# Chunked attention and a sine MLP on one core: two stages one after the other, rewritten as an interleaved sequence

## The chip, the cores and the metric

The kernel runs on one NeuronCore of a Trainium2 chip. The metric is device time in microseconds (us) of one execution, taken over several runs; beside it stands one profiled execution, whose trace gives each instruction's start and duration on the engines: PE (TensorE, matrix products; PEld is its loading of weights), ACT (ScalarE, activation functions and copies), DVE (VectorE, elementwise work), POOL (GpSimd, here memsets, copies and the issue of DMAs) and SP (SyncE, the issue of DMAs).

## What is computed

Four batches, eight heads, 768 positions, head size 64. Queries are taken in chunks of 32; a chunk sees the keys from 16 positions before it to 8 behind it, and 8 memory keys of its head. The attention's output, 3072 tokens of 512 features, goes through a two-layer network with a sine in the middle.

```python
for c in range(24):                               # chunks of 32
    q_c = q[:, :, 32*c : 32*c+32]
    k_full = concat([mem_k, k[:, :, max(0, 32*c-16) : min(768, 32*c+40)]])
    v_full = concat([mem_v, v[:, :, max(0, 32*c-16) : min(768, 32*c+40)]])
    a = exp(q_c @ k_full.T / 8 - max); a = a / a.sum()
    out[:, :, 32*c : 32*c+32] = a @ v_full
x = out as 3072 x 512
h = x @ w_in                                      # 512 -> 2048
g = h + sin(alpha * h)**2 / alpha
y = g @ w_out                                     # 2048 -> 512
```

Inputs and output are float32; the products run in bfloat16.

## The kernel before

Work on the attention goes by blocks of 96 queries, three chunks; 96 queries see 120 keys, which with the 8 memory keys are exactly 128 partitions. So one product of a 128-column window of `kTi` (keys, transposed) with 96 columns of `qT_all` (queries, transposed) gives the scores of one head and block with the keys on the partitions. Which of the three chunks may see which key is put in by six more rows of the contraction: rows 64 to 69 of `qT_all` and `kTi` hold patterns (`qft`, `kgit`, built in lines 69 to 124) whose product adds 256 where a key is allowed, and the Exp (L237) takes 32 away again after scaling.

`prep_head` (L147 to L219) loads one head of one batch in float32, most of it from SP, the middle of the values from POOL (L204, L208, L214). VectorE casts queries and keys (L157, L177, L178); TensorE transposes them in pieces of 128 or 96 (L160, L180, L183 to L185) into two PSUM tiles `t1`, `t2`; ScalarE copies them out (L161, L186, L190, L194); VectorE copies the memory keys (L195) and the pattern rows (L165, L199) and casts the values (L218). `attn_block` (L221 to L260) does a block: per four heads four score products (L231), one Exp of 384 columns (L237), four products with the values (L244), a reciprocal and a multiplication (L248, L249), then four transposes to put features on the partitions (L257) and a copy into `xT_store` (L260), which holds all 3072 tokens.

Behind the four batches comes the MLP, in six blocks of 512 tokens. For each of 16 tiles of 128 hidden features: four matmuls (L303) into `hT`, Sin on ScalarE (L310), the square on ScalarE (L316) or VectorE (L320) in turn, and the last step on VectorE (L323), which reads `hT` again. `hT` has three buffers. Then, for each 128 tokens, 16 matmuls (L331), a copy by ScalarE (L338) and a store from SP (L339).

The order of the instructions on each engine is set by the Tile scheduler, from priorities that follow the program's order. The MLP's pools are opened only when the attention's are closed, so its PSUM is the attention's PSUM.

Of the kernel before, what the change touches and what calls it, by code (L numbers as in the profile page):

```python
# [9 lines left out]
CHUNK = 32  # L10
BIG = 256.0
EXP_BIAS = -32.0
P = 128
QW = 96


def _bf16_tile(pool, shape, name, **kw):
    return pool.tile(shape, mybir.dt.bfloat16, name=name, **kw)


def _f32_tile(pool, shape, name, **kw):
    return pool.tile(shape, mybir.dt.float32, name=name, **kw)
# [3 lines left out]
def kernel(  # L26
# [16 lines left out]
    assert D == 64 and H * D == d_model and d_model == 512 and d_ff % P == 0  # L43
    assert S % QW == 0 and S % P == 0 and S % 192 == 0 and NM == 8
    NJ = S // QW
    NQB = S // P
    NTOK = B * S
    FT = d_ff // P
    KT = d_model // P
    NPOS = S  # L50
    KCOLS = 16 + NPOS + 8 * 9
    NSEG = 9
    scale = 1.0 / 8.0

    consts = ctx.enter_context(tc.tile_pool(name="consts", bufs=1))

    ident = _bf16_tile(consts, [P, P], "ident")
    masks.make_identity(nc, ident[:])

    bias_exp = _f32_tile(consts, [P, 1], "bias_exp")  # L60
    nc.vector.memset(bias_exp[:], EXP_BIAS)

    qft = _bf16_tile(consts, [P, NPOS], "qft")
    kgit = _bf16_tile(consts, [P, KCOLS], "kgit")

    tmp_stack = ExitStack()
    pattmp = tmp_stack.enter_context(tc.tile_pool(name="pattmp", bufs=1))

    qf0 = _bf16_tile(pattmp, [6, NPOS], "qf0")
    nc.gpsimd.memset(qf0[:], 0.0)  # L70
    qf_view = qf0[:].rearrange("p (a m r) -> p a m r", a=NPOS // 192, m=6, r=32)
    nc.gpsimd.affine_select(
        out=qf_view, in_=qf_view, compare_op=mybir.AluOpType.not_equal,
        fill=BIG, base=0, pattern=[[0, NPOS // 192], [1, 6], [0, 32]],
        channel_multiplier=-1,
    )
    kg0 = _bf16_tile(pattmp, [6, NPOS], "kg0")
    nc.gpsimd.memset(kg0[:], 0.0)
    kg_view = kg0[:].rearrange("p (a u) -> p a u", a=NPOS // 192, u=192)
    nc.gpsimd.affine_select(  # L80
        out=kg_view, in_=kg_view, compare_op=mybir.AluOpType.is_ge, fill=1.0,
        base=-40, pattern=[[0, NPOS // 192], [1, 192]], channel_multiplier=-32,
    )
    nc.gpsimd.affine_select(
        out=kg_view, in_=kg_view, compare_op=mybir.AluOpType.is_ge, fill=0.0,
        base=16, pattern=[[0, NPOS // 192], [1, 192]], channel_multiplier=-32,
    )
    kgC = kg0[:, 192:NPOS].rearrange("p (a u) -> p a u", a=NPOS // 192 - 1, u=192)
    nc.gpsimd.affine_select(
        out=kgC, in_=kgC, compare_op=mybir.AluOpType.is_ge, fill=1.0,  # L90
        base=152, pattern=[[0, NPOS // 192 - 1], [1, 192]], channel_multiplier=-32,
    )
    kgD = kg0[:, 0:NPOS - 192].rearrange("p (a u) -> p a u", a=NPOS // 192 - 1, u=192)
    nc.gpsimd.affine_select(
        out=kgD, in_=kgD, compare_op=mybir.AluOpType.is_gt, fill=1.0,
        base=176, pattern=[[0, NPOS // 192 - 1], [-1, 192]], channel_multiplier=32,
    )
    kgi = _bf16_tile(pattmp, [6, KCOLS], "kgi")
    nc.gpsimd.memset(kgi[:], 0.0)
    nc.vector.tensor_copy(kgi[:, 16:24], kg0[:, 0:8])  # L100
    for s in range(1, 8):
        nc.vector.tensor_copy(
            kgi[:, 32 + 104 * (s - 1):32 + 104 * (s - 1) + 96],
            kg0[:, 8 + 96 * (s - 1):8 + 96 * s],
        )
    nc.vector.tensor_copy(kgi[:, 760:848], kg0[:, 680:768])
# [263 lines left out]
```

## Time and profile before

| | us |
|---|---|
| median of 3 runs | 392.58 |
| lowest, highest | 391.58, 392.81 |
| span of the profiled execution, first to last instruction | 391.8 |
| PE busy in it | 300.2 |
| DVE busy | 230.6 |
| ACT busy | 199.4 |
| POOL busy | 78.1 |

No separate time is listed for the profiled execution; its span is 391.8, 0.8 below the median of the runs, and that much is taken to lie around it. How to read what follows: in a group, `L310 ACT ACTIVATE u<-hT,alpha_sb` is the instruction of line 310 on ScalarE that writes `u` from `hT` and `alpha_sb`, with shapes and count; then busy us, mean ns of one, then the engine's idle time just before them and what ended it. A timeline row has start, duration, engine, line, and how many are merged. A row of windows has, for a stretch, the busy time and count of PE, PEld, DVE, ACT and POOL, the granted clock, the mean busy share of the DMA engines, and GB/s. DMA rows have the size and the median time from issue to landing. `SPq` and `POOLq` are the queues from which SP and POOL issue.

### The profile page before, as it was taken

The page shows a single profiled execution, that of the slowest core. Times are in us where ns is not written, and L with a number is a line of the kernel's source. Part 1 is how long each engine was busy: PE and PEld are TensorE (multiplying, and loading weights), DVE is VectorE, ACT ScalarE, POOL GpSimd, SP SyncE. Part 2 cuts the span into 40 slices and gives each one's busy share as a digit, 9 for nine tenths or more (in the row PEclk, how much of TensorE's full clock was granted, in tenths as well). Part 3 has the DMA queues.
Part 4 walks back from the last instruction along what each step waited for, and adds up shares of the span by engine and source line. Part 5 has one row for each costly group of instructions (what it writes and reads, how often), then busy time and mean ns, then how long its engine had stood idle before and what let it go on. Part 6 is the DMA issues. An engine that isn't in the chain of part 4 may idle for free.

```text
span 391.8 us, 5738 instructions
## 1 busy us (share of the span) xinstructions
PE 300.2 (77%) x1908; PEld 177.6 (45%) x1924; DVE 230.6 (59%) x707; ACT 199.4 (51%) x362; POOL 78.1 (20%) x115
## 2 busy tenths in 40 slices
PE   0245543975577956598588999999999999999996
PEld 0134432853455734486474344444444444444442
DVE  6988213578455788467273970880870870871860
ACT  0334442643446634474554863863863763763761
POOL 9835302003453442624100000000000000000000
PEclk9999999999999999999999999999999999999999
DMA  5977999913597455855200002002002002002002
GB/s 134 174 133 123 205 194 190 155 31 72 117 174 133 90 104 124 152 114 119 43 2 0 0 2 105 3 3 107 0 2 107 0 2 107 1 2 108 0 13 96
DMA packets 66989, 31.73 MB, mean 81 GB/s; under 512 B 59152, under 2 KB 61200, under 8 KB 66960
## 3 DMA queue, kind: packets, MB, share of 16 engines
q1 hardware_dynamic: 60272, 19.75, 24.7%
q0 software_dynamic: 6688, 11.62, 14.4%
q8 instruction: 15, 0.25, 0.3%
q14 instruction: 14, 0.11, 0.1%
HBM read 29.24 MB, written 6.29 MB: 91 GB/s over the span
## 4 chain that ended last, share of the span: by engine, by line
PE 51%; ACT 17%; DVE 13%; DMA 9%; issue 4%; POOL 3%; SPq 2%; another core or an unknown queue 0%; DVEq 0%; ACTq 0%; POOLq 0%
PE ops_t L331 19%; PE hT L303 12%; ACT u L310 5%; DMA k_stage<-in_k_dram 5%; PE out L244 5%; DVE gT L323 4%; DMA v_stage<-in_v_dram 4%; PE t L160 4%; ACT s L316 4%; PE t L183 4%; PE ps L231 3%; ACT kTi L190 2%; ACT qT_all L161 2%; ACT pT L237 2%; PE xtp L257 2%
## 5 line engine op out<-in xcount | busy, mean ns | idle before, releaser
L323 DVE SCALAR_TENSOR_TENSOR gT<-s,inv_alpha,hT 128x512 bf16<-128x512 f32 x96 | 71.2, 747 | 63.7 <-ACT s L316 61.5
L303 PE MATMUL hT<-xT_store,w_in_sb 128*128 128x512 bf16 x375 | 94.8, 385 | 5.6 <-DVE gT L323 3.6
L331 PE MATMUL ops_t<-w_out_sb,gT 128*128 128x512 bf16 x377 | 89.3, 379 | 0.4
L310 ACT ACTIVATE u<-hT,alpha_sb 128x512 f32<-128x512 f32 x96 | 64.6, 679 | 18.4 <-PE hT L303 16.6
L303 PEld LDWEIGHTS <-w_in_sb 128*128 128x128 bf16 x384 | 38.0, 99 | 56.2 <-issue 15.7
L331 PEld LDWEIGHTS <-gT 128*128 128x128 bf16 x384 | 37.0, 98 | 46.2 <-DVE gT L323 4.7
L160 PE MATMUL t<-ident,q_bf 128*64 128x128 bf16 x192 | 26.2, 309 | 24.1 <-DVE kTi L195 21.8
L161 ACT COPY qT_all<-t 64x768 bf16<-64x768 bf16 x32 | 25.3, 792 | 36.4 <-PE t L160 36.3
L237 ACT ACTIVATE pT<-ps,bias_exp 128x384 bf16<-128x384 f32 x64 | 35.4, 577 | 14.9 <-PE ps L231 11.3
L244 PE MATMUL out<-Vwin,pT 128*96 128x65 bf16 x256 | 35.1, 269 | 7.6 <-ACT pT L237 5.3
L204 POOL DMA_DIRECT2D v_stage<-in_v_dram x32 | 21.5, 671 | 95.0 <-DVE Vwin L218 59.3
L338 ACT COPY o_sb<-ops_t 128x512 f32<-128x512 f32 x24 | 14.0, 585 | 49.8 <-PE ops_t L331 47.6
L231 PE MATMUL ps<-qT_all,kTi 70*128 70x96 bf16 x256 | 35.9, 276 | 3.5 <-DVE kTi L195 2.0
L320 DVE TENSOR_TENSOR s<-u 128x512 f32<-128x512 f32 x48 | 32.8, 684 | 5.0 <-ACT u L310 5.0
L190 ACT COPY kTi<-t 64x576 bf16<-64x576 bf16 x32 | 20.2, 632 | 25.8 <-PE t L185 25.8
L160 PEld LDWEIGHTS <-q_bf 128*64 128x64 bf16 x192 | 20.9, 162 | 27.6 <-issue 20.1
L244 PEld LDWEIGHTS <-pT 128*96 128x96 bf16 x256 | 28.0, 188 | 11.1 <-ACT pT L237 8.9
L208 POOL DMA_DIRECT2D v_stage<-in_v_dram x32 | 28.5, 889 | 14.2 <-DMA w_out_sb<-in_moe_w_out_dram 12.7
L316 ACT ACTIVATE s<-u 128x512 f32<-128x512 f32 x48 | 30.2, 630 | 1.5
L180 PE MATMUL t<-ident,k_bf 96*64 96x96 bf16 x64 | 10.9, 270 | 25.3 <-DVE k_bf L178 13.8
L231 PEld LDWEIGHTS <-kTi 70*128 70x128 bf16 x256 | 23.9, 137 | 8.6 <-issue 4.3
L183 PE MATMUL t<-ident,k_bf 96*64 96x96 bf16 x192 | 20.9, 276 | 7.9 <-ACT kTi L186 7.6
(59 smaller groups left out, 275.8 us busy)
## 6 DMA issues: line engine op xcount, KB each, us to landing
q_stage<-in_q_dram SPq DMA_DIRECT2D x32, 192.0 KB
out_dram<-o_sb SPq DMA_DIRECT2D x24, 256.0 KB
k_stage<-in_k_dram SPq DMA_DIRECT2D x32, 168.0 KB
v_stage<-in_v_dram POOLq DMA_DIRECT2D x32, 168.0 KB, 4.2
w_in_sb<-in_moe_w_in_dram POOLq DMA_DIRECT2D x1, 2048.0 KB, 15.8
w_out_sb<-in_moe_w_out_dram POOLq DMA_DIRECT2D x1, 2048.0 KB, 28.7
v_stage<-in_v_dram POOLq DMA_DIRECT2D x32, 42.0 KB, 3.0
k_stage<-in_k_dram SPq DMA_DIRECT2D x32, 22.0 KB
```

The source lines that it names most:

```text
L160: nc.tensor.transpose(t1[:, jb, :], q_bf[:, jb, :], ident[:])
L161: nc.scalar.copy(qT_all[0:64, h, 0:NPOS].rearrange("p (j c) -> p j c", j=NQB), t1[:, 0:NQB, :],)
L183: nc.tensor.transpose(t2[:, s - 3, 0:QW], k_bf[:, s, :], ident[0:QW, 0:QW])
L231: nc.tensor.matmul(ps4[:, e, :], kTi[0:70, h, 104 * j:104 * j + P], qT_all[0:70, h, QW * j:QW * j + QW],)
L237: nc.scalar.activation(pT4[:], ps4[:], mybir.ActivationFunctionType.Exp, bias=bias_exp[:], scale=scale,)
L244: nc.tensor.matmul(og[0:QW, e, :], pT4[:, e, :], Vwin[:, h, j, :])
L303: nc.tensor.matmul(hT[:, :], w_in_sb[:, kt, ft * P:(ft + 1) * P], xT_store[:, kt, tokbase:tokbase + TB], start=(kt == 0), stop=(kt == KT - 1),
L310: nc.scalar.activation(u[:], hT[:], mybir.ActivationFunctionType.Sin, scale=alpha_sb[:, ft:ft + 1],)
L316: nc.scalar.activation(s2[:], u[:], mybir.ActivationFunctionType.Square,)
L320: nc.vector.tensor_tensor(out=s2[:], in0=u[:], in1=u[:], op=mybir.AluOpType.mult,)
L323: nc.vector.scalar_tensor_tensor(out=gT[:, ft, :], in0=s2[:], scalar=inv_alpha[:, ft:ft + 1], in1=hT[:], op0=mybir.AluOpType.mult, op1=myb ...
L331: nc.tensor.matmul(ops_t[:, :], gT[:, ft, s * P:(s + 1) * P], w_out_sb[:, ft, :], start=(ft == 0), stop=(ft == FT - 1),)
```

## The change

The kernel is rewritten; line numbers of the new one are given here as N.

- Order. `tc.manual_schedule()` makes each engine run its instructions in the order in which the code writes them. Attention of batch 0 comes first ("burst"). Then, for each batch i, the first product of its MLP ("L1": 16 tiles over all 768 tokens, N297 to N318), and after it the attention of batch i+1 mixed with the second product of batch i ("L2", N320 to N339). L2 is a Python generator that yields after each matmul; `Stream.take(n)` emits n of them. Within a burst, a step emits the scores and Exps of one block, then some matmuls of L2, the product with the values of an earlier block (1 block earlier, 4 in the first mixed burst, 2 in batch 0's), more of L2, and the transposes of the block before that. What is left of L2 goes two matmuls per tile into the next L1, and the rest behind it.
- Preparation. Loads cast from float32 to bfloat16 on the way and are all issued from POOL. Two heads lie side by side: VectorE puts a pair together (`pair_up`, N193), one transpose of 128 by 128 serves both, six for keys (`t_k`) and six for queries (`t_q`) of a pair; position 6a+r of a head comes out as column a of transpose r, so the copies out of PSUM read with a step of 128 elements. The queries go to `qz`, whose first half has the odd head's rows at zero and whose second half the even head's, so that one product with 192 columns gives both heads' scores. The preparation of batch i+1 is written into L1 of batch i, one half pair every second tile.
- Masks. The pattern rows go. Each block has three Exps, one per chunk of 32 queries for all eight heads (256 columns), with a bias per partition that is -30000 for keys that the chunk does not see (`biasm`).
- Values. They are loaded by block and not by head, two DMAs for a block, into `vws`; the memory rows are copied in by POOL (`put_memv`), the memory keys likewise (`put_memk`).
- PSUM. `big`, two buffers of two banks, serves scores and `hT` (now 128 by 768, two halves of 384); `opp`, one bank, the output of L2; `atp`, three banks, the rest. In the last L2 every second output tile takes a bank of `atp`.
- MLP. L1 has 8 matmuls of 384 columns per tile; the square is on VectorE in every second tile of batch 0 and in every fourth of the others. The outputs are copied in turn by VectorE and ScalarE.
- Weights. `w_in` comes in eight DMAs and `w_out` in four, behind the values of batch 0.

PE, in the attention of a later batch. Before, scores and value products stand among the transposes of the next batch's preparation (`t` tiles):

```order
L184 MATMUL t_2114<-ident,k_bf 64x24
L185 LDWEIGHTS memk_bf
L185 MATMUL t_2114<-ident,memk_bf 64x8
L257 LDWEIGHTS x_blk
L257 MATMUL xtp<-ident,x_blk 128x96
```

Now, in the second burst: `sc` are the scores, `o` the output of L2 of the batch before, `ot` the product with the values.

```order
L233 MATMUL sc<-qz,kTi 128x192
L327 LDWEIGHTS gT
L327 MATMUL o<-w_out_sb,gT 128x512
L327 LDWEIGHTS gT
L327 MATMUL o<-w_out_sb,gT 128x512
L327 LDWEIGHTS gT
L327 MATMUL o<-w_out_sb,gT 128x512
L261 LDWEIGHTS pt_99
L261 MATMUL ot<-vw_88,pt_99 128x65
```

Matmuls of the MLP now stand between those of the attention.

POOL, near the start. Before, its share of the value loads begins among the pattern constants:

```order
L112 AFFINE_SELECT sel<-sel 6x70 [waits Pool_49]
L204 DMA v_stage<-in_v_dram 24x7x64
L89 AFFINE_SELECT kg_75<-kg_75 6x576 [waits Pool_49]
L208 DMA v_stage<-in_v_dram 96x7x64
L94 AFFINE_SELECT kg_75<-kg_75 6x576 [waits Pool_49]
L214 DMA v_stage<-in_mem_v_dram 8x8x64
```

Now the values (`vw`) stand behind the memory keys, which wait for VectorE's copy of the last transposes:

```order
L134 COPY kTi<-memkT 128x8x8 [waits DVE_49]
L134 COPY kTi<-memkT 128x8x8 x3
L116 DMA vw_88<-in_v_dram 48x8x64 [waits DMASW5_49]
L120 DMA vw_88<-in_v_dram 56x8x64 [waits DMASW6_49]
L127 COPY vw_88<-memv_st 8x8x64 [waits DMASW4_49,Pool_49]
L127 COPY vw_88<-memv_st 8x8x64 x7
L116 DMA vw_88<-in_v_dram 64x8x64 [waits DMASW7_49]
```

and behind the last of them the weights, and the keys and queries of batch 1:

```order
L120 DMA vw_88<-in_v_dram 48x8x64 [waits DMASW4_49]
L181 DMA w_in_sb<-in_moe_w_in_dram 128x4x256 [waits DMASW5_49]
L181 DMA w_in_sb<-in_moe_w_in_dram 128x4x256 [waits DMASW6_49]
L181 DMA w_in_sb<-in_moe_w_in_dram 128x4x256 [waits DMASW7_49]
L181 DMA w_in_sb<-in_moe_w_in_dram 128x4x256 [waits DMASW0_49]
L181 DMA w_in_sb<-in_moe_w_in_dram 128x4x256 [waits DMASW1_49]
L181 DMA w_in_sb<-in_moe_w_in_dram 128x4x256 [waits DMASW2_49]
L181 DMA w_in_sb<-in_moe_w_in_dram 128x4x256 [waits DMASW3_49]
L181 DMA w_in_sb<-in_moe_w_in_dram 128x4x256 [waits DMASW4_49]
L106 DMA k_bf<-in_k_dram 128x8x384 [waits DMASW5_49]
L106 DMA q_bf<-in_q_dram 128x8x384 [waits DMASW6_49]
```

All loads but `alpha`'s stand in this one queue, and from the ninth on each waits for the one eight places ahead of it to land.

DVE, in the MLP. Before, only squares and last steps:

```order
L320 TENSOR_TENSOR s_3471<-u 128x512 [waits Activation_49]
L323 SCALAR_TENSOR_TENSOR gT<-s_3471,inv_alpha,hT 128x512 [waits DVE_49]
L323 SCALAR_TENSOR_TENSOR gT<-s_3481,inv_alpha,hT 128x512 [waits Activation_49]
L320 TENSOR_TENSOR s_3491<-u 128x512 [waits Activation_49]
L323 SCALAR_TENSOR_TENSOR gT<-s_3491,inv_alpha,hT 128x512 [waits DVE_49]
```

Now, at the beginning of L1 of batch 0, the pair-ups (`pr`) of batch 1 stand between them and wait for their loads:

```order
L314 SCALAR_TENSOR_TENSOR gT<-s_607,inv_alpha,hT 128x768 [waits DVE_49,PE_49]
L195 COPY pr<-k_bf 128x2x6x64 [waits DMASW5_49]
L314 SCALAR_TENSOR_TENSOR gT<-s_623,inv_alpha,hT 128x768 [waits PE_49,Activation_49]
L195 COPY pr<-q_bf 128x2x6x64 [waits DMASW6_49]
L210 COPY kTi<-tk 128x48 [waits Activation_49]
L210 COPY kTi<-tk 128x48
L311 TENSOR_TENSOR s_649<-u 128x768 [waits Activation_49]
L314 SCALAR_TENSOR_TENSOR gT<-s_649,inv_alpha,hT 128x768 [waits DVE_49,PE_49]
```

The core of the new code:

```diff
+    def put_memk(b):
+        for hp in range(HP):
+            nc.gpsimd.tensor_copy(
+                kTi[:, hp, 24:KW].rearrange("p (j c) -> p j c", c=104)[:, :, 40:40 + NM],
+                memkT[:, hp, NM * b:NM * b + NM].unsqueeze(1).to_broadcast([P, NJ, NM]),
+            )
...
+    def pair_up(src, hp):
+        pr = blk.tile([P, 6, 2, D], BF, name="pr")
+        nc.vector.tensor_copy(
+            pr[:].rearrange("p r e d -> p e r d"), src[:, 2 * hp:2 * hp + 2]
+        )
+        return pr
...
+    def t_q(qb, hp):
+        t = atp.tile([P, 6, P], BF, name="tq", tag="at")
+        for r in range(6):
+            nc.tensor.transpose(t[:, r, :], qb[:, r].rearrange("p e d -> p (e d)"), ident[:])
+        nc.scalar.copy(
+            qz[0:64, hp, 0, :].rearrange("p (a r) -> p a r", r=6),
+            t[0:64].rearrange("p r a -> p a r"),
+        )
+        nc.vector.tensor_copy(
+            qz[64:128, hp, 1, :].rearrange("p (a r) -> p a r", r=6),
+            t[64:128].rearrange("p r a -> p a r"),
+        )
...
+    def burst(b, stream, shares, lag):
+        xT = xp.tile([P, KT, S], BF, name="xT")
+        ptl, xbl = {}, {}
+        for s in range(NJ + lag + 1):
+            n = shares[s] if s < len(shares) else 0
+            if s < NJ:
+                ptl[s] = qk_exp(s)
+            stream.take(n // 2)
+            if 0 <= s - lag < NJ:
+                xbl[s - lag] = pv(b, s - lag, ptl.pop(s - lag))
+            stream.take(n - n // 2)
+            if 0 <= s - lag - 1 < NJ:
+                xt(xT, s - lag - 1, xbl.pop(s - lag - 1))
+        return xT
...
+    def l1(i, ft, xT, gT, dve_sq):
+        hT = big.tile([P, 2, 512], F32, name="hT", tag="big")
+        for kt in range(KT):
+            for hf in range(2):
+                nc.tensor.matmul(
+                    hT[:, hf, 0:HALF],
+                    w_in_sb[:, kt, P * ft:P * ft + P],
+                    xT[:, kt, HALF * hf:HALF * hf + HALF],
+                    start=(kt == 0), stop=(kt == KT - 1),
+                )
...
+    xT = burst(0, empty, (), 2)
+    stream = empty
+    for i in range(B):
+        gT = gp.tile([P, FT, S], BF, name="gT")
+        last = i == B - 1
+        for ft in range(FT):
+            dve_sq = (ft % 2 == 1) if i == 0 else (ft % 4 == 3)
+            l1(i, ft, xT, gT, dve_sq)
+            if not last:
+                pc = {2: 0, 4: 1, 6: 2, 8: 3, 10: 4, 12: 5, 14: 6, 15: 7}.get(ft)
+                if ft == 1:
+                    prs = pair_up(kq_next[0], 0)
+                if pc is not None:
+                    now = prs
+                    if pc < 7:
+                        prs = pair_up(kq_next[(pc + 1) % 2], (pc + 1) // 2)
+                    (t_k if pc % 2 == 0 else t_q)(now, pc // 2)
+            if 1 <= ft:
+                stream.take(2)
+        if not last:
+            put_memk(i + 1)
+        stream.take(200)
+        stream = Stream(l2(i, gT, last))
+        if not last:
+            if i + 2 < B:
+                kq_next = load_qk(i + 2)
+            shares = (0, 5, 5, 6, 6, 6, 6, 6, 6, 6, 6, 6, 6)
+            xT = burst(i + 1, stream, shares, 4 if i == 0 else 1)
```

488 lines of the change are left out of this document (229 added, 259 removed).

## Prediction

> **What bounds the kernel now.** I read the page first, then the busy time by stretches, cut where the work changes kind, then the timeline and the chain of waits inside each stretch. From the page:
>
> ```profile
> span 391.8 us, 5738 instructions
> ...
> PEclk9999999999999999999999999999999999999999
> ```
>
> The stretches are the pattern constants, the attention of all four batches, and the MLP (PE, PEld, DVE, ACT, POOL):
>
> ```profile
> 0.00:13.00 13.00, 1.72 (x4) 0.62 (x5) 9.47 (x43) 0.00 (x0) 12.33 (x24) 1.00 0.73 148
> 13.00:210.80 197.80, 126.93 (x1152) 102.13 (x1152) 121.03 (x521) 93.19 (x193) 65.77 (x92) 1.00 0.65 118
> 210.80:391.80 181.00, 171.59 (x752) 74.84 (x767) 100.14 (x144) 106.20 (x169) 0.00 (x0) 1.00 0.10 35
> ```
>
> In the MLP TensorE is busy 171.6 of 181.0 us: it is the bound. In the attention no engine is; there 198 us go in waits between engines. The two stretches lie one after the other, and the first leaves TensorE, the second ScalarE and VectorE, half idle. The timeline shows something the clock row does not:
>
> ```profile
> 24.84 0.80 PE L160 MATMUL t<-ident,q_bf 128*64 128x128 bf16 x6 [1.03 <-DVE kTi L195]
> ...
> 211.62 4.29 PE L303 MATMUL hT<-xT_store,w_in_sb 128*128 128x512 bf16 x10 [0.22 <-issue]
> ```
>
> Ten matmuls of 512 columns take 4.29 us just after the attention, 0.43 us each. The chain of waits has the same work later, one pass of the MLP's first product, and ahead of them the load of the Sin table (the row that names no tile):
>
> ```profile
> 212.75 1.28 ACT L310
> 214.04 1.27 ACT u L310 x2
> ...
> 242.69 0.88 PE hT L303 x4
> ...
> 243.60 0.70 ACT u L310
> ...
> 244.32 0.64 ACT s L316
> ...
> 244.98 0.76 DVE gT L323
> ...
> 245.78 1.02 PE hT L303 x4
> ...
> 377.16 7.58 PE ops_t L331 x35
> ...
> 388.06 0.59 ACT o_sb L338
> ```
>
> 35 matmuls in 7.58 us are 0.217 us each: twice as fast, though the clock row says 9 throughout. So the attention runs TensorE at half rate, and continuous work brings the full rate after some 4 us.
>
> **What goes and what stays.** TensorE's 1152 small instructions of the attention become 708: 196 transposes instead of 512, 128 query products instead of 256, and 256 and 128 as before. VectorE loses the casts and the copies of the mask rows, ScalarE half of its copies; one Exp of 384 becomes, per block, three of 256 for twice the heads. The MLP's matmuls keep their columns: 512 of 384 and 384 of 512 are 393,216, as 768 of 512 were. All of this leaves a stretch that no engine bounds, so the busy times saved there count for nothing by themselves; what counts is how the new stretches chain.
>
> **What each operation costs.** Groups, with mean ns of one after the comma:
>
> ```profile
> L323 DVE SCALAR_TENSOR_TENSOR gT<-s,inv_alpha,hT 128x512 bf16<-128x512 f32 x96 | 71.2, 747 | 63.7 <-ACT s L316 61.5
> L310 ACT ACTIVATE u<-hT,alpha_sb 128x512 f32<-128x512 f32 x96 | 64.6, 679 | 18.4 <-PE hT L303 16.6 <-remote 1.3
> L237 ACT ACTIVATE pT<-ps,bias_exp 128x384 bf16<-128x384 f32 x64 | 35.4, 577 | 14.9 <-PE ps L231 11.3 <-PE out L244 2.8
> L320 DVE TENSOR_TENSOR s<-u 128x512 f32<-128x512 f32 x48 | 32.8, 684 | 5.0 <-ACT u L310 5.0
> L249 DVE TENSOR_TENSOR x_blk<-out,rinv 96x256 bf16<-96x256 f32 x64 | 25.5, 414 | 0.3
> L161 ACT COPY qT_all<-t 64x768 bf16<-64x768 bf16 x32 | 25.3, 792 | 36.4 <-PE t L160 36.3
> L190 ACT COPY kTi<-t 64x576 bf16<-64x576 bf16 x32 | 20.2, 632 | 25.8 <-PE t L185 25.8
> L165 DVE COPY qT_all<-qft 6x768 bf16<-6x768 bf16 x32 | 13.1, 409 | 0.5
> L260 DVE COPY xT_store<-xtp 128x384 bf16<-128x384 bf16 x32 | 11.3, 354 | 15.0 <-PE xtp L257 14.8
> L120 DVE CAST qft<-pq 6x512 bf16<-6x512 f32 x1 | 0.7, 689 | 0.0
> L120 DVE CAST qft<-pq 6x256 bf16<-6x256 f32 x1 | 0.4, 412 | 0.0
> ```
>
> ScalarE's slope is (792-632)/192 = 0.83 ns per element, VectorE's out of PSUM (689-412)/256 = 1.08. So at 768 columns: Sin 679+213 = 0.89 us, Square 0.64+0.21 = 0.85, the last step 747+277 = 1.02, a VectorE square 684+277 = 0.96; an Exp of 256 is 577-107 = 0.47. A 672-column copy on ScalarE is 632+80 = 0.71. VectorE's strided query copy is 0.412+512*1.08/1000 = 0.97 at one element a cycle, and 0.35+0.20 = 0.55 if it keeps L260's rate; I take 0.95, as its elements are not neighbours. The two edge copies of 48 elements are 0.14+0.05 each by the same rows, 0.36 together. A pair-up is 0.41 by L165.
>
> **The new L1 phase (16 tiles, one batch).** TensorE has 8 matmuls of 384 columns per tile, 8*0.163 = 1.30 us. But there are two `big` buffers, and one is free again only after 1.30+0.89+0.85+1.02 and four handovers of 0.03, 4.2 us: one tile per 2.1 us. TensorE with two matmuls of L2 (0.43) and half a group of transposes (0.4 at most) is inside that; ScalarE has 0.89+0.75*0.85+(0.71+0.79)/4 = 1.90, VectorE 1.02+0.25*0.96+0.41/2+(0.36+0.95)/4 = 1.79. All three stand close to 2.1, in fixed order, so copies get in front of a Sin: I take 2.3 with the preparation, 2.15 without. That is 36.8 and 34.4 us, against 16*1.30 = 20.8 if TensorE bounded it.
>
> **The new attention (burst).** The small matmuls before:
>
> ```profile
> 201.75 0.53 PE L244 MATMUL out<-Vwin,pT 128*96 128x65 bf16 x4
> ...
> 204.29 0.51 PE L231 MATMUL ps<-qT_all,kTi 70*128 70x96 bf16 x4
> ```
>
> Four take 0.53 and 0.51 with some 0.27 for the last to come through, so 0.08 us lie between them. A block has 4 query matmuls (192 columns, 0.10 each at full rate), 8 of values and 4 transposes (0.075): 1.3 us, eight blocks 10.4. With 52 matmuls of L2 (11.3), 2.0 until the first Exps are through behind the table load, 0.9 at each of three output tiles (one `opp` buffer, emptied by a copy that TensorE waits for), and 1.2 for the last block's VectorE work: 27.6. The first interleaved burst has 70 of L2 and four output tiles: 32.4. Three Exps a block, 1.41 us, stay under TensorE's 2.6.
>
> Table loads go from two to eight, six more: 7.7 us by the 1.28 of the chain. The three for Exp sit in the 2.0 above; those for Sin run while ScalarE waits for the last `xT`, 1.2 us of VectorE work, and cost nothing unless that cover shrinks. [...] In the chain the first Sin starts 0.01 us behind the load, so the trace shows no drain after it, and I keep 1.28.
>
> **The start.** POOL and VectorE rows, and landing times:
>
> ```profile
> L208 POOL DMA_DIRECT2D v_stage<-in_v_dram x32 | 28.5, 889 | 14.2 <-DMA w_out_sb<-in_moe_w_out_dram 12.7 <-issue 1.4
> ...
> L168 DVE MEMSET k_stage<- 16x64 f32 x32 | 3.6, 112 | 1.2
> ...
> L219 DVE MEMSET Vwin<- 128x8 bf16 x32 | 2.0, 65 | 1.6
> ...
> L72 POOL TENSOR_SCALAR_AFFINE_SELECT qf<-qf 6x768 bf16<-6x768 bf16 x1 | 1.0, 1007 | 0.0
> ...
> L99 POOL MEMSET kgi<- 6x856 bf16 x1 | 0.8, 802 | 0.0
> ```
>
> ```profile
> v_stage<-in_v_dram POOLq DMA_DIRECT2D x32, 168.0 KB, 4.2
> w_in_sb<-in_moe_w_in_dram POOLq DMA_DIRECT2D x1, 2048.0 KB, 15.8
> w_out_sb<-in_moe_w_out_dram POOLq DMA_DIRECT2D x1, 2048.0 KB, 28.7
> ```
>
> VectorE's memsets (4,400 elements a lane by the listed shapes, at (112-65)/56 = 0.84 ns, and twenty starts of 0.06) end near 6 us. Four head pairs follow in series on VectorE: two pair-ups 0.8, then it waits for six transposes (0.8) and the ScalarE copy 0.71, edges 0.36, the other ScalarE copy, its own 0.95: 3.8 us, 15.2 in all, 21 us. Memory keys to 22.8. POOL waits for them, and behind them stand all value loads: 2 issues (0.82), eight copies of 512 elements (0.48 by L99, 0.67 by L72, I take 0.55), 14 issues: 17.5, so the last issue is at 39.5, landed by 43.7, and 2.7 us of value product and transposes later, at 46.5, L1 of batch 0 begins. Before, nothing of this waited: SP issued most loads.
>
> Then comes the worst place. `w_in`, keys and queries of batch 1 queue on POOL after the values. `w_out` was issued one POOL issue, 0.8 us, behind `w_in`, so 28.7+0.8-15.8 = 13.7 us passed between their landings: 4.2 MB of float32 in 14 us; `w_in`, from 41, then occupies the queue to 55, keys to 60, queries to 65.5, landed by 67. VectorE meets its pair-up of batch 1 after two tiles and stands; behind it queue that phase's last steps, and behind those TensorE. Three tiles by 67, then 13 at 2.25: L1 ends at 96.3. Without the wait, 82.5. Behind the queries stand `w_out` (to 80) and the values of batch 1, whose last issues and copies come near 96 as well, with the memory keys of batch 1 at the end of the same queue: a slower queue would hold the next burst too. In later batches POOL's loads and copies have a whole L1 phase, 36.8 us, and cost nothing.
>
> **The sum.** 96.3 + burst 32.4 + L1 36.8 + burst 27.6 + L1 36.8 with 14 left matmuls and an output tile (3.9) + burst 27.6 + L1 34.4 + 3.9 + L2 of the last batch 96*0.217 = 20.8 + 3.8 after the last matmul (391.8-388.0) = 324.3. The median of the runs, 392.58, is 0.8 over the profiled span, so 325; 326 with a microsecond for a slow clock after the waits. The old MLP needed 167 us of matmul at full rate; that remains. What goes is most of 198 us of attention alone; what comes back is TensorE waiting some 8 to 15 us in each L1 phase, and the start.
>
> **The rivals.**
> A: L1 costs less and loads come early. Per tile 2.1 instead of 2.25 and 2.3 (-9), no wait at output tiles (-9), keys and queries there 8 us sooner: 300. For it: 2.1 is the bare chain; against: three engines near 1.9 in fixed order.
> B: strided copies and loads cost double. ScalarE and VectorE now read PSUM at steps of 128 elements; no row has that. At twice 0.75 us, eight copies per L1 add 6 us, thrice 18, the start 6; value loads in rows of 64 elements, cast on the way, could double their 13 us for 8 more on the path: 326+32 = 358.
> C: slower than before. TensorE at half rate in L1, since it no longer runs unbroken:
>
> ```profile
> 160.00:180.00 20.00, 16.62 (x165) 14.14 (x165) 11.16 (x53) 12.62 (x27) 8.24 (x12) 1.00 0.66 130
> ...
> 215.90:377.20 161.30, 156.00 (x694) 68.50 (x707) 97.21 (x141) 99.96 (x160) 0.00 (x0) 1.00 0.09 33
> ```
>
> and in the first of these stretches the chain has
>
> ```profile
> 163.27 0.86 PE t L160 x6
> ```
>
> Half rate was seen at 83% busy (six transposes as slow as at 24.84), full rate at 97%; L1 would have 1.30+0.43+0.2 of 2.3, 84%. Then a tile takes 2.6+0.86+0.3 = 3.75, four phases 23 us more each: 418. It turns slower from 66 us, so if more than 72% of L1 runs so. Against it: the 83% were small matmuls, six transposes or four products between waits, while L1's are 384 and 512 wide with gaps under 1 us. [...]
> That the change doesn't do what it says is excluded by the listed order: L2's matmuls stand between the attention's.
>
> **How the numbers follow.** Forecast 326, own range 312 to 340: 0.55. A 0.17, B 0.22, C 0.06. The range 298 to 364 leaves out C, and the outer third of A and of B: 0.06+0.13. Within 0.3% (1.2 us, about what a measurement here can tell from no change) only C could land: 0.01. Slower 0.05, faster 0.94.
>
> **What would show it.** Right: VectorE standing at the first pair-up of batch 1 for its load; L1 phases of 35 to 38 us with TensorE waiting for the last step; `o` matmuls at 0.217 in the bursts; L1 of batch 0 from 45 to 50. Wrong: L1 phases near 22 us or over 42, L2 matmuls at 0.43, the values' loads not last at the first attention, or a burst over 32 us after the first.

## The result, and the profile after

| | us |
|---|---|
| changed kernel, median of 4 runs | 310.91 (310.78 to 313.27) |
| kernel before, beside it, median of 4 | 392.69 (391.58 to 393.56) |
| ratio, 95% interval | 0.793 (0.790 to 0.796) |
| span of the profiled execution | 309.2 |

The forecast was 326, its sum 324.3 of span: the direction and the stages are there, 15 us less in all. The time lies 1 us under the forecast's own range of 312 to 340 and inside the wider one of 298 to 364, nearer to rival A (300) than to the forecast. The ratios further down leave out slow executions, one each of three_big, three_big_b and two_early_mid, while the times in us are medians of all. From here on, line numbers are those of the changed kernel. The page, in its busy shares, the granted clock and the chain:

```profile
span 309.2 us, 4313 instructions
...
PE 228.8 (74%) x1604; PEld 130.5 (42%) x1604; DVE 169.6 (55%) x358; ACT 169.9 (55%) x256; POOL 92.5 (30%) x163
...
PEclk9999959699986999999989999999999999999999
...
PE 43%; DVE 21%; ACT 18%; POOL 7%; issue 5%; DMA 4%; DVEq 0%; ACTq 0%
```

TensorE still stands for a quarter of the span. Where, the busy time by stage shows; the cuts are at the first matmul of a phase (PE, PEld, DVE, ACT, POOL, granted clock, DMA share, GB/s):

```profile
0.00:43.07 43.07, 19.31 (x181) 14.48 (x181) 22.64 (x81) 17.60 (x34) 33.54 (x69) 0.96 0.79 73
43.07:92.41 49.34, 28.43 (x181) 16.77 (x180) 31.97 (x45) 27.64 (x33) 27.61 (x42) 0.88 1.17 148
92.41:119.55 27.14, 24.45 (x197) 13.82 (x197) 12.49 (x42) 11.89 (x27) 13.19 (x24) 0.90 0.80 94
119.55:159.94 40.39, 30.81 (x204) 17.78 (x204) 27.49 (x41) 31.17 (x38) 3.81 (x5) 0.99 0.20 34
159.94:181.35 21.41, 19.07 (x179) 11.47 (x179) 12.40 (x42) 11.30 (x26) 14.37 (x26) 0.94 1.07 118
181.35:221.65 40.30, 35.07 (x221) 19.35 (x221) 27.49 (x41) 30.00 (x37) 0.00 (x0) 1.00 0.04 14
221.65:244.17 22.52, 18.19 (x182) 10.93 (x180) 12.45 (x42) 13.17 (x28) 0.00 (x0) 1.00 0.13 47
244.17:283.89 39.72, 32.63 (x172) 16.62 (x171) 20.57 (x21) 25.34 (x30) 0.00 (x0) 1.00 0.04 14
283.89:309.20 25.31, 20.88 (x96) 9.30 (x95) 2.08 (x3) 1.76 (x3) 0.00 (x0) 1.00 0.19 73
```

| stage | forecast | measured |
|---|---|---|
| start and burst 0 | 46.5 | 43.1 |
| L1 of batch 0 | 49.8 | 49.3 |
| burst 1 | 32.4 | 27.1 |
| L1 of batch 1 | 36.8 | 40.4 |
| burst 2 | 27.6 | 21.4 |
| L1 of batch 2, with the left matmuls | 40.7 | 40.3 |
| burst 3 | 27.6 | 22.5 |
| L1 of batch 3, with the left matmuls | 38.3 | 39.7 |
| L2 of the last batch, end | 24.6 | 25.3 |

The three interleaved bursts are 16.6 us shorter than forecast, the start 3.4; the L1 phases together are 4.1 longer. One block of burst 2, on TensorE:

```profile
169.64 0.49 PE L233 MATMUL sc<-qz,kTi 128*128 128x192 bf16 x4
169.98 0.81 PE L327 MATMUL o<-w_out_sb,gT 128*128 128x512 bf16 x3
170.62 0.41 PE L261 MATMUL ot<-vw,pt 128*128 128x65 bf16 x8
170.87 0.81 PE L327 MATMUL o<-w_out_sb,gT 128*128 128x512 bf16 x3
171.51 0.34 PE L275 MATMUL xtp<-ident,x_blk 96*128 96x96 bf16 x4
171.69 0.41 PE L233 MATMUL sc<-qz,kTi 128*128 128x192 bf16 x3
```

No row has an idle time at its end: TensorE runs without a gap, 2.05 us a block. Up to the next row's start, six matmuls of L2 take 1.28 of that, four query products 0.34, eight value products 0.25 and four transposes 0.18: the attention's sixteen small ones are 0.77, where the forecast had 1.3. Groups that answer to other prices:

```profile
L301 PE MATMUL hT<-xT,w_in_sb 128*128 128x384 bf16 x512 | 95.4, 332 | 24.2 <-DVE gT L314 22.8 <-DVE xT L278 0.9
L327 PE MATMUL o<-w_out_sb,gT 128*128 128x512 bf16 x384 | 102.6, 387 | 10.7 <-DVE o_sb L335 6.8 <-ACT o_sb L337 3.9
L223 DVE COPY qz<-tq 64x768 bf16<-64x768 bf16 x16 | 15.4, 961 | 1.9 <-ACT qz L219 1.6
L120 POOL DMA_DIRECT2D vw<-in_v_dram x32 | 23.3, 728 | 13.6 <-DMA q_bf<-in_q_dram 9.0 <-DMA w_out_sb<-in_moe_w_out_dram 3.9 <-DMA w_in_sb<-in_moe_w_in_dram 0.7
L116 POOL DMA_DIRECT2D vw<-in_v_dram x32 | 22.0, 687 | 7.9 <-DMA w_out_sb<-in_moe_w_out_dram 4.2 <-DMA k_bf<-in_k_dram 3.2 <-DMA w_in_sb<-in_moe_w_in_dram 0.6
```

Ahead of `hT` TensorE waits for the last step (`gT`), ahead of `o` for the copy of the output tile, as forecast. The strided query copy takes 0.96, as taken (0.95). In the chain of waits, the stand in L1 of batch 0:

```profile
44.11 12.74 DMA k_bf<-in_k_dram
...
57.30 0.82 PE tk L203 x6
58.12 2.44 PE hT L301 x8
```

and one pass of the two-buffer chain in L1 of batch 1:

```profile
126.64 1.31 PE hT L301 x8
...
127.97 0.91 ACT u L308
...
128.91 0.97 DVE s L311
...
129.97 1.02 DVE gT L314
...
131.04 1.48 PE hT L301 x8
```

One pass is 4.4 us for two tiles, 2.2 a tile.

### The profile page after: what moved, and what is told of

It is laid out like the page before. It is cut to its first block, busy times and chain, and to the rows that moved or that the text cites. A ratio compares the mean times of both kernels' runs of the same rounds, so it can differ in the third digit from the quotient of the medians.

```text
span 309.2 us, 4313 instructions
## 1 busy us (share of the span) xinstructions
PE 228.8 (74%) x1604; PEld 130.5 (42%) x1604; DVE 169.6 (55%) x358; ACT 169.9 (55%) x256; POOL 92.5 (30%) x163
## 4 chain that ended last, share of the span: by engine, by line
PE 43%; DVE 21%; ACT 18%; POOL 7%; issue 5%; DMA 4%; DVEq 0%; ACTq 0%
PE o L327 22%; PE hT L301 15%; ACT u L308 8%; DVE gT L314 8%; ACT s L313 5%; DMA k_bf<-in_k_dram 4%; DVE s L311 4%; PE sc L233 2%; DVE qz L223 2%; DVE o_sb L335 2%; POOL w_in_sb L181 2%; POOL vw L120 2%; PE tk L203 2%; PE ot L261 2%; ACT o_sb L337 2%
## 5 line engine op out<-in xcount | busy, mean ns | idle before, releaser
L301 PE MATMUL hT<-xT,w_in_sb 128*128 128x384 bf16 x512 | 95.4, 332 | 24.2 <-DVE gT L314 22.8
L327 PE MATMUL o<-w_out_sb,gT 128*128 128x512 bf16 x384 | 102.6, 387 | 10.7 <-DVE o_sb L335 6.8
L314 DVE SCALAR_TENSOR_TENSOR gT<-s,inv_alpha,hT 128x768 bf16<-128x768 f32 x64 | 64.8, 1013 | 44.0 <-ACT s L313 39.8
L308 ACT ACTIVATE u<-hT,alpha_sb 128x768 f32<-128x768 f32 x64 | 57.7, 901 | 50.2 <-PE hT L301 49.9
L247 ACT ACTIVATE pt<-sc,biasm 128x256 bf16<-128x256 f32 x96 | 37.9, 477 | 29.4 <-PE sc L233 29.4
L327 PEld LDWEIGHTS <-gT 128*128 128x128 bf16 x384 | 35.4, 99 | 39.7 <-issue 15.1
L313 ACT ACTIVATE s<-u 128x768 f32<-128x768 f32 x44 | 37.1, 843 | 1.4
L265 DVE TENSOR_TENSOR x_blk<-ot,rinv 96x256 bf16<-96x256 f32 x64 | 26.9, 421 | 2.2
L120 POOL DMA_DIRECT2D vw<-in_v_dram x32 | 23.3, 728 | 13.6 <-DMA q_bf<-in_q_dram 9.0
L233 PE MATMUL sc<-qz,kTi 128*128 128x192 bf16 x128 | 18.9, 283 | 8.9 <-DVE qz L223 6.0
L116 POOL DMA_DIRECT2D vw<-in_v_dram x32 | 22.0, 687 | 7.9 <-DMA w_out_sb<-in_moe_w_out_dram 4.2
L311 DVE TENSOR_TENSOR s<-u 128x768 f32<-128x768 f32 x20 | 19.2, 958 | 6.3 <-ACT u L308 6.0
L204 ACT COPY kTi<-tk 128x672 bf16<-128x672 bf16 x16 | 11.3, 707 | 18.2 <-PE tk L203 18.2
```

Of the source, the lines that this page charges most:

```text
L116: nc.gpsimd.dma_start(vw[r0:64, :, j, 0:D], v[b, :, lo + r0:lo + 64, :].rearrange("h p d -> p h d"))
L120: nc.gpsimd.dma_start(vw[72:72 + n, :, j, 0:D], v[b, :, QW * j + 48:QW * j + 48 + n, :].rearrange("h p d -> p h d"),)
L233: nc.tensor.matmul(sc[:, hp // 2, 192 * (hp % 2):192 * (hp % 2) + 192].rearrange("p (e c) -> p e c", e=2), kTi[:, hp, 104 * j:104 * j + P] ...
L247: nc.scalar.activation(pt[:, 0:H * QW].rearrange("p (g e c) -> p g e c", g=2, e=4)[:, :, :, 32 * m:32 * m + 32], sc[:, :, 0:4 * QW].rearra ...
L265: nc.vector.tensor_tensor(out=x_blk[:, 4 * g:4 * g + 4, :], in0=ot[0:QW, :, 0:D], in1=rinv[:, 4 * g:4 * g + 4].unsqueeze(2).to_broadcast([ ...
L301: nc.tensor.matmul(hT[:, hf, 0:HALF], w_in_sb[:, kt, P * ft:P * ft + P], xT[:, kt, HALF * hf:HALF * hf + HALF], start=(kt == 0), stop=(kt ...
```

## Experiments

Three reasons were open: what bounds a burst, what bounds L1, and what the start is made of. A ratio is to the kernel before, in runs on the same chip, with its 95% interval; 0.010 is 3.9 us. The changed kernel has 0.793.

### The interleaving taken out: serial

```diff
-            if 1 <= ft:
-                stream.take(2)
...
-            shares = (0, 5, 5, 6, 6, 6, 6, 6, 6, 6, 6, 6, 6)
+            stream.take(200)
+            shares = ()
```

> The second product of a batch runs in one piece between its L1 phase and the next burst; no matmul of it stands in a burst or an L1 phase. Theory (what the trace of the changed kernel suggests: in the interleaved burst TensorE has no gap, 6 matmuls of 0.217 and 0.74 of small ones a block, while VectorE has 1.5 and ScalarE 1.2): a burst alone is bound by VectorE and the waits between engines, some 1.9 per block, 15.2 + 4.5 at the ends = 20 us, against 27, 21 and 22 interleaved. L1 keeps its 36 to 37. Sum: 43.8 + 48.6 + 3 x (20.9 + 20 + 36.7) + 20.9 + 4.4 = 350 us. Rival 1 (the old attention's half rate comes back when no wide matmul stands between the small ones): small matmuls at twice the time, burst at 25 or more, 365 or more. Rival 2 (the bursts were bound by TensorE and shrink to its 0.74 a block): bursts of 12, 326 us.

Measured: 351.97 us in its one run, span 350.0. The sum hit, two of its terms did not. The stretch of the first lone burst, and rows of TensorE from it:

```profile
114.56:131.97 17.41, 11.81 (x129) 9.33 (x128) 10.17 (x39) 12.22 (x27) 0.76 (x4) 0.74 0.05 16
```

```profile
119.00 0.49 PE L233 MATMUL sc<-qz,kTi 128*128 128x192 bf16 x4 [0.60 <-ACT pt L247]
...
122.69 0.84 PE L233 MATMUL sc<-qz,kTi 128*128 128x192 bf16 x4
...
128.03 0.33 PE L275 MATMUL xtp<-ident,x_blk 96*128 96x96 bf16 x4
```

This burst takes 17.4 us, the later ones some 15 (from their first query products at 195.0 and 273.1 to the first `hT` at 209.6 and 287.7), not 20; L2 alone takes 25, not 20.9, since TensorE stands at each output tile for its copy. The two errors cancel. The price of the interleaving is what the pair was made for: 352 against 311, 41 us, about half of the 82 us that the rewrite gained. Rival 1 is half seen: the first query products still run at full rate (0.49 for four), all small matmuls from 119.5 to 126.3 at half rate (0.84), and the next ones at full rate again (0.33 for four transposes), so in this burst lone small matmuls neither keep the full rate nor stay slow by themselves. Rival 2 (326) fell.

### What a small matmul costs in a burst: double_qk

```diff
-            nc.tensor.matmul(
...
+            for _ in range(2):
+                nc.tensor.matmul(
...
```

> The changed kernel with every query product issued twice into the same place, 32 matmuls of 192 columns more per burst, 128 in all. What one small matmul costs in an interleaved burst: by the forecast's price (0.10 for the columns and 0.08 between, taken from the attention before) 0.18 x 96 = 17 us over the three interleaved bursts, 328 us, ratio 0.835. By the trace of the changed kernel (0.49 for four, with the last one's way out; 0.081 between two at full rate) 0.081 x 96 = 7.8 us, 319 us, ratio 0.813. If TensorE does not bound the bursts: 0 to 2 us, ratio under 0.799. The burst of batch 0 waits for loads and takes it up in each case.

Measured: 316.53 us, ratio 0.803 (0.800 to 0.805): 0.0096 more, 3.8 us. One set of query products in it, on TensorE's timeline:

```profile
105.01 0.83 PE L234 MATMUL sc<-qz,kTi 128*128 128x192 bf16 x8
105.68 0.59 PE L328 MATMUL o<-w_out_sb,gT 128*128 128x512 bf16 x2
```

Eight take 0.83 with the last one's way out, and the next matmul follows 0.67 after the first of them began: 0.084 each. So 0.18 is refuted as a price. It is not what the forecast's sum used either: the 1.3 of a block is 4 x 0.10 + 12 x 0.075, so the query products were nearly right there, and the price of value products and transposes, which this run does not vary, was off. The 3.8 us (some 2 to 5 by the two intervals) are half of 7.8, as if about half of a burst's blocks lay on the path. In burst 3 the products of the first two blocks lie beside the wait for the first Exps, and at an output tile the wait shrinks instead (0.59 us in the changed kernel at 230.71, 0.26 here at 235.34). So "TensorE bounds the bursts" holds for their middle, not for all of them.

### The start: early_values, kq_mid

```diff
+    load_v(0, 0)
+    put_memv(0)
+    for j in range(1, 2):
+        load_v(0, j)
     put_memk(0)
-    for j in range(NJ):
+    for j in range(2, NJ):
         load_v(0, j)
-        if j == 0:
-            put_memv(0)
```

> POOL issues the value loads of two blocks and copies the memory values of batch 0 before its copies of the memory keys, for which it stood waiting 7.67 us. Theory (the start, and the wait for keys and queries of batch 1, are set by POOL's queue): everything behind comes 7.3 us earlier: last value issue at 30.4 instead of 37.7, keys and queries issued at 37 instead of 44, landed at 50 instead of 57; L1 of batch 0 begins at 39 to 40 and ends 7 earlier: 303.5 us. Rival (the DMA engines, not the issues, set when keys and queries land; the first burst is bound by its own chain): L1 of batch 0 begins 2 to 4 us earlier, keys land within 3 us of 57: 308 to 310 us.

Measured: 306.09 us, ratio 0.775 (0.770 to 0.781), 0.018 or 7.0 us less. In its chain of waits:

```profile
30.70 5.88 POOL w_in_sb L181 x8
36.58 13.04 DMA k_bf<-in_k_dram
```

Everything behind POOL's wait comes 7 us earlier, the landing of the keys (49.6 instead of 56.9) too. L1 of batch 0 begins at 36.5. POOL's queue was on the path; the rival falls. kq_mid is this, and also:

```diff
-    for c in range(8):
+    for c in range(2):
         load_w_in(c)
     kq_next = load_qk(1)
+    for c in range(2, 8):
+        load_w_in(c)
```

> early_values, and the loads of keys and queries of batch 1 issued behind two of the eight pieces of w_in instead of behind all. Theory (they land late for the bytes queued ahead of them): they land near 42 instead of 50, VectorE's stand at the first pair-up goes, L1 of batch 0 ends 6 us earlier: 298 us where early_values had a ratio of 0.775 (304.4 on the 392.7 of the kernel before), ratio 0.760. Rival (the loads share the DMA engines with what is queued behind them, and the pieces of w_in come late in their stead): TensorE waits for w_in, gain under 2 us, ratio 0.771 or more.

Measured: 297.24 us, ratio 0.755 (0.751 to 0.759), a further 0.0205 or 8 us. The first transposes of batch 1 now begin at 45.2, not 50.1. With the stand of 6.2 us ahead of them goes the half rate behind it, at which sixteen `hT` took 4.81 in early_values. What the rival said is there, but small: TensorE's two waits for `w_in` are 1.5 us together, the longer 0.9.

### What bounds L1: three_big, three_big_b, take3

A third pair of banks for `hT`; in the bursts it holds a block's value products, and transposes keep one bank (at the start, those of the queries use `big`).

```diff
-    atp = ctx.enter_context(tc.tile_pool(name="atp", bufs=3, space=bass.MemoryType.PSUM))
+    bxp = ctx.enter_context(tc.tile_pool(name="bxp", bufs=1, space=bass.MemoryType.PSUM))
+    atp = ctx.enter_context(tc.tile_pool(name="atp", bufs=1, space=bass.MemoryType.PSUM))
...
-        hT = big.tile([P, 2, 512], F32, name="hT", tag="big")
+        if ft % 3 == 2:
+            hT = bxp.tile([P, 2, 512], F32, name="hT", tag="bx")
+        else:
+            hT = big.tile([P, 2, 512], F32, name="hT", tag="big")
...
+        ot2 = bxp.tile([P, 2, 512], F32, name="ot", tag="bx")
         for g in range(2):
-            ot = atp.tile([P, 4, D + 1], F32, name="ot", tag="at")
+            ot = ot2[:, g, 0:4 * (D + 1)].rearrange("p (e c) -> p e c", e=4)
```

> A third two-bank PSUM buffer for hT (every third tile), which in the bursts holds the value products of a block; transposes keep one bank. Theory (L1 is paced by the chain of two buffers, 4.2 to 4.4 us for two tiles): a tile falls from 2.3 to what the busiest engine has, 1.9 to 2.0, so L1 phases from about 36.5 to 31, four times: 288 us, the bursts as before or 1 us longer each (one bank for transposes). Rival (three engines near 1.9 in fixed order set 2.3, the buffers only look guilty): L1 phases stay at 35 to 37, and the time stays within 4 us of 311.

Measured: 320.81 us, ratio 0.813 (0.807 to 0.818), slower by 8. Its groups, its L1 of batch 3 and its waits:

```profile
L306 PE MATMUL hT<-xT,w_in_sb 128*128 128x384 bf16 x512 | 96.0, 333 | 1.9 <-DVE xT L280 0.9 <-DVE gT L319 0.7 <-DMA w_out_sb<-in_moe_w_out_dram 0.3
```

```profile
258.42:287.80 29.38, 27.00 (x155) 15.13 (x155) 18.54 (x20) 24.21 (x29) 0.00 (x0) 1.00 0.03 10
```

```profile
PE ot L263 <- DVE x_blk L267: 23.2, 32, 0.7
```

TensorE's wait for the last step goes from 22.8 us to 0.7: the buffers did cause it. L1 of batch 3, the one without a preparation, is 29.4 us to its last tile, where the changed kernel takes 35.4, and TensorE is busy in 27.0 of it. But the L1 phases with a preparation fall by only 1.5 (batch 1 from 37.5 to 36.0 up to the first query products, batch 2 from 36.7 to 35.2 up to the left matmuls), though TensorE no longer waits there for a last step either. In its L1 of batch 1 it waits instead for pair-ups (1.8) and for copies that empty the one bank left to the transposes (3.0). So in these phases the time is set by the preparation; how much of that is VectorE's fixed order, as the rival has it, and how much the bank that this variant took away, was not separated. And the bursts lost more than L1 gained, 0.7 us in each of 32 blocks, because in the shared buffer the second group's products waited for the division of the first. three_big_b mends that:

```diff
         for g in range(2):
             ot = ot2[:, g, 0:4 * (D + 1)].rearrange("p (e c) -> p e c", e=4)
...
+        for g in range(2):
+            ot = ot2[:, g, 0:4 * (D + 1)].rearrange("p (e c) -> p e c", e=4)
             nc.vector.reciprocal(rinv[:, 4 * g:4 * g + 4], ot[0:QW, :, D])
```

> three_big with the value products of both groups issued ahead of both divisions (in three_big TensorE stood 0.73 us between the two groups of every block). Theory (three_big lost its gain there, in bursts of 33, 29 and 27 us instead of 27, 21 and 22): bursts as in the changed kernel, L1 phases as in three_big (41, 39, 41 with its leftover piece, 33 with its own): 310.9 - 2 - 7 = 302 us, ratio to the kernel before 0.77. Rival (one bank pair for a block's value products holds the next block up until both divisions are done): bursts stay at 25 or more, 312 us or more.

Measured: 300.64 us, ratio 0.762 (0.758 to 0.766), 12 us under the changed kernel. Only its times are used here. Then the slack of TensorE in L1:

```diff
-                stream.take(2)
+                stream.take(3 if i >= 2 else 2)
```

> In the L1 phases of batches 2 and 3 three matmuls of the second product stand behind each tile, not two, so that none is left over behind the phase. Theory (chain-bound L1: TensorE waits there anyway): the two leftover pieces of 3.63 us go, the phases themselves stay: 303.5 us. Rival (TensorE, at 1.30 + 0.65 + 0.2 a tile, comes onto the path or delays the next tile's products behind it): each phase grows by 15 x 0.217 = 3.3 us, nothing is gained: 310 us.

Measured: 315.54 us, ratio 0.800 (0.797 to 0.803), 2.7 us slower, worse than the rival's price. TensorE's waits in its L1 of batch 2:

```profile
PE o L327 <- DVE o_sb L335: 3.5, 1, 3.5
PE sc L233 <- DVE qz L223: 2.1, 1, 2.1
PE hT L301 <- DVE gT L314: 1.3, 3, 1.0
```

The wait for the last step is small (3.6 in the changed kernel). In its place TensorE stands once for 3.5 us at an output tile, whose copy stands behind a last step, a pair-up and two edge copies in VectorE's queue, and the burst's first query products now wait 2.1 for the last query copy, which the left matmuls had covered; behind them it runs at half rate up to 229.9 (three `o` in 1.47). The gain was turned into two new waits.

### Output tiles, and all together: two_out, three_early_mid, two_early_mid

```diff
-    opp = ctx.enter_context(tc.tile_pool(name="opp", bufs=1, space=bass.MemoryType.PSUM))
-    atp = ctx.enter_context(tc.tile_pool(name="atp", bufs=3, space=bass.MemoryType.PSUM))
+    opp = ctx.enter_context(tc.tile_pool(name="opp", bufs=2, space=bass.MemoryType.PSUM))
+    atp = ctx.enter_context(tc.tile_pool(name="atp", bufs=2, space=bass.MemoryType.PSUM))
```

> Two banks for the output tiles of the second product instead of one, two instead of three for the attention's and the transposes. Theory (as in the forecast, TensorE stands at each output tile for its copy; the trace of the changed kernel has 0.6 to 0.8 there, seven times in bursts, and 1.4 at most in L1): 5 to 7 us go: 305 us, ratio 0.777. Rival (with two banks the second group of values and the transposes wait for VectorE's division, 0.3 us a block, 24 blocks): no gain or up to 5 us slower, 311 to 316.

Measured: 303.47 us, ratio 0.769 (0.765 to 0.773), 9.5 us. Its group of `o`:

```profile
L327 PE MATMUL o<-w_out_sb,gT 128*128 128x512 bf16 x384 | 100.8, 385 | 0.0
```

All of the 10.7 us of waiting for output copies is gone, and with 9.5 us less in time most of it was on the path. The rival's wait is there too, but small: transposes wait 3.6 us in all for VectorE's division, most of it in the burst of batch 0, which grows from 21.4 to 23.3 us. The combinations:

> three_big_b, early_values and kq_mid together. Theory (third buffer, POOL queue and load order each take away a wait of their own): the gains add, 310.9 - 9 - 7 - 6 = 289 us, ratio 0.736. Rival (they take away the same stand of the first L1 phase in part, and TensorE, now without gaps in L1, is the bound): 294 to 298, ratio 0.75 to 0.76.

> two_out, early_values and kq_mid together. Theory (the waits for output tiles lie in bursts and late L1 phases, those for loads in the start and the first L1 phase, so nothing is paid twice): the ratios' gains add, 0.769 - 0.018 - 0.021 = 0.730, 287 us. Rival (the chain of two hT buffers takes back part, as its slack is used): 0.74 or more, 291 us.

Measured: three_early_mid 288.80 us, 0.733 (0.730 to 0.737); two_early_mid 292.45 us, 0.740 (0.737 to 0.743). Against the parts as measured, each sum falls short by 0.009, 3.6 us. The traces show one place for it: the burst of batch 0, which has no L2 beside it, takes 14.8 us in kq_mid (first query product 22.5, first `hT` 37.3), but 18.2 in three_early_mid (22.0 to 40.2) and 17.7 in two_early_mid (22.0 to 39.7), where transposes and value products wait for a bank. Without the early loads the lost bank cost 1.9 us there (two_out).

### The ends of L1: two_tail, three_tail

```diff
-                pc = {2: 0, 4: 1, 6: 2, 8: 3, 10: 4, 12: 5, 14: 6, 15: 7}.get(ft)
+                pc = {2: 0, 4: 1, 6: 2, 8: 3, 10: 4, 12: 5, 13: 6, 14: 7}.get(ft)
...
-            shares = (0, 5, 5, 6, 6, 6, 6, 6, 6, 6, 6, 6, 6)
+            shares = (4, 5, 5, 6, 6, 6, 6, 6, 6, 6, 6, 6, 6)
```

> two_early_mid, with the last two transposes of a preparation one tile earlier (tiles 13 and 14 instead of 14 and 15) and four matmuls of the second product in the burst's first step, where none stood. Theory (the first query product of a burst waits 2 to 3.5 us for the last query copy, and TensorE then stands for the first Exps): 1 to 2 us a burst from each, 5 us in all: ratio 0.717. Rival (VectorE's queue at the end of L1 is as long either way, and the four matmuls are only moved from the end of the burst to its beginning): under 1.5 us, 0.727 or more.

> three_early_mid with the same two edits as two_tail. Theory: 5 us as there, from 0.733 to 0.720, 283.5 us. Rival: under 1.5 us, 0.730 or more.

Measured: two_tail 287.05 us, 0.727 (0.724 to 0.729), 5.2 us better than two_early_mid; three_tail 289.54 us, 0.734 (0.733 to 0.736), no better than three_early_mid. The group of `o` in two_tail and in three_tail:

```profile
L327 PE MATMUL o<-w_out_sb,gT 128*128 128x512 bf16 x361 | 94.4, 379 | 1.2
```

```profile
L334 PE MATMUL o<-w_out_sb,gT 128*128 128x512 bf16 x361 | 96.1, 380 | 16.0 <-DVE o_sb L342 11.1 <-ACT o_sb L344 3.8
```

With one output bank, waiting for output copies grows from 12.0 to 16.0 us, 4.0 that would offset a gain of the size seen in two_tail; with two banks there is nothing to wait for. Which of the two edits brings the 5 us was not tested. In the traces of two_early_mid and two_tail, the wait of query products for VectorE falls from 6.0 to 3.4 us, that of value products for Exps from 2.6 to 1.2, and the stretch at half rate at the beginning of burst 2 (three `o` in 1.47) is gone. two_tail is the fastest version of the study, 27% under the kernel before and 8% under the change.

## Why the prediction was right, and where its sizes were off

- **MLP bound by TensorE, attention at half rate before.** Right. `o` matmuls run at 0.216 in most of the bursts (three in 0.64 up to the next matmul), L1's at 0.164 (eight in 1.31). The forecast's sign of being wrong, L2 matmuls at 0.43, shows only at the beginning of two bursts, in the first ten `o` of burst 1 and the first two of burst 2:

```profile
93.16 2.34 PE L327 MATMUL o<-w_out_sb,gT 128*128 128x512 bf16 x5
```

Rival C did not come: TensorE's stands of up to 1.8 us within L1 leave the rate as it is, while after the stand of 7.0 us that ends at 57.30 eight `hT` take 2.44 instead of 1.31. In that stand the granted clock falls to 0.50 at 53.4 us, 3.1 us after its beginning at 50.3. How long a stand brings a fall is not shown: at 39.8 us the clock falls too, and no stand ahead of that is longer than 1.0 us (last section).
- **The price of a block in a burst (1.3 us).** The step that failed in size. The 1.3 is four query products at 0.10 and twelve value products and transposes at 0.075. "0.08 us lie between them" was read from the attention before, which ran at half rate, and the 0.075 was used unscaled in bursts at full rate. Measured, a value product is 0.03, a transpose 0.04, a query product of 192 columns 0.08, and a block 0.77. Eight blocks, 0.53 each: 4.2 us a burst, 13 of the 16.6 us. From start to start, a product of 96 columns took 0.08 us in the attention before (four in 0.31 at 204.29), and one of 192 columns 0.084 at full rate (double_qk), about half the time per column.
- **Output-tile waits (0.9 each), Exp ramp (2.0).** In place, somewhat smaller: in burst 3, for one, TensorE stands 0.59, 0.67 and 0.84 us at its three output tiles. two_out shows that most of them were on the path.
- **L1 paced by two `hT` buffers and fixed order (2.3 and 2.15 a tile).** Sizes right: 36.7 us from 181.35 to the left matmuls at 218.04, 35.4 without preparation. The mechanism is right for the last phase (three_big); in the others the preparation takes the buffers' place once a third one is there. Missing was the end of L1 of batch 1: the next burst's query products wait for the last query copy, which stands behind the last step on VectorE; with an output copy in mid-phase it made 40.4 of 36.8. In batch 2 the left matmuls cover it. TensorE stood 21, 10, 5 and 7 us in the four phases, where the forecast had 8 to 15 in each.
- **The start (46.5).** Right in kind: POOL waits 7.67 us for the memory keys and the value issues follow. An issue takes 0.69 or 0.73, not 0.82, 1.8 us in sixteen; the first value issue came at 22.0, not 22.8, and L1 began 6.0 us behind the last one, not 7.0.
- **The wait for keys and queries of batch 1.** Right: VectorE stood for its load. Keys and queries were used at 56.9 and 60.7, 3 and 6 us sooner than taken, but the 13 tiles behind took 31.7 us, 2.44 each and not 2.25: the first at half rate, and at the end 3.5 us of waiting for the last query copy. kq_mid prices the order of these loads at 8 us.
- **Table loads hidden.** For Sin, yes: the four loads, 1.28 us each, end 0.2 to 3.2 us before the first matmul into `hT` of their phase. For Exp mostly: behind the loads ahead of bursts 1 and 2 ScalarE stands another 1.5 and 0.9 us for the query products; ahead of burst 3 one is on the chain, behind an output copy,

```profile
222.30 1.28 ACT L247
...
223.59 0.47 ACT pt L247
```

and the Exp follows 0.01 us behind it.
- **Rival A (300)** was nearly right on the loads and wrong on L1 and on the output tiles. That the time came to lie nearer to it than to the forecast is luck: the bursts made the difference, and it had left them alone. **Rival B** fell: strided reads and value loads cost no more than taken. ScalarE's copies of 672 and 768 columns take 0.71 and 0.78 us (0.71 and 0.79 taken), VectorE's 0.96 (0.95), and a value load lands 3.4 or 3.5 us behind its issue, in the median, where the forecast had 4.2 from the kernel before.

## What to carry to other kernels

A price read from rows that ran at half rate must be scaled before it is used in a stage that runs at full rate: here 0.075 us for value products and transposes that took 0.03 and 0.04 made most of the error. After a rewrite that fills one engine, ask of each queue what its first wait holds up: two reorderings on POOL, of loads and of the copies beside them, brought 15 us without a change to what any engine computes. When TensorE runs nearly without gaps, see what an edit makes of the waits for output copies: the same two edits brought 5 us with two output banks (two_tail) and nothing with one (three_tail).

## What the runs showed of the hardware

The granted clock falls in places, with one core at work: its mean is 0.961 in the profiled run of the changed kernel. In the changed kernel's trace the records of the clock begin at 36.38 us, and each but the last lasts 3.41 us or a multiple of it. Two of its falls, each with the stretch of 3.41 us ahead:

```profile
36.38:39.79 3.41, 1.94 (x34) 1.44 (x31) 2.60 (x11) 3.20 (x7) 3.41 (x5) 1.00 1.42 89
39.79:46.62 6.83, 6.10 (x37) 3.12 (x36) 3.40 (x13) 1.02 (x2) 5.72 (x9) 0.50 1.25 154
...
87.58:90.99 3.41, 1.32 (x14) 0.91 (x13) 2.25 (x6) 2.62 (x3) 2.68 (x4) 1.00 1.31 202
90.99:97.82 6.83, 5.41 (x19) 2.84 (x19) 1.33 (x2) 3.75 (x10) 4.97 (x8) 0.50 1.73 178
```

The first fall comes in the sparse end of burst 0, 3.3 us before L1 begins at 43.07: eight value products take 0.90 at 40.90, where they took 0.40 at 38.50, and the first sixteen `hT` 4.57 instead of 2.77. The full rate is back 3.5 us after L1 began. In serial it falls in the same way at 119.5, behind a stretch with 0.98 us of work, and at 129.8, behind one with 2.35 us of small matmuls; its first lone burst's last transposes and then fifteen `hT` (4.54) run at half rate. How much work in a stretch keeps the rate stays open: behind the 1.60 us from 84.17 to 87.58, most of it in matmuls of 384 columns, it stayed at 1.00, and behind 1.94 or 2.35 of small ones it fell. The first fall costs 1.8 us in the sixteen `hT` behind it (4.57 against 2.77).

The half rate of the attention before need not be another thing, though the clock row shows 1.00 there. The records of that trace begin at 215.6 us, where the rate rises; for the time ahead of it there is no record. It is the same here before 36.38, with four query products in 0.84 at 34.26 beside a row of 1.00. So the rate is to be read from the matmuls until the first record.
